# Sixteen-point Fourier stages as packed 64x64 matmuls, with the filter tables stored in halves by frequency

## The chip, the cores and the metric

The kernel runs on one core of a Trainium2 chip. Its metric is the device time of one execution in microseconds (us). The kernel before took 217.96 us, the median of three runs from 217.56 to 218.0. One execution was recorded by the hardware profiler: 218.46 us as a run, of which 216.3 us are the span from its first recorded instruction to its last. TensorE had its full clock (1.00) as the mean of that span.

## What is computed

The input x has 2048 rows of 640 values in bf16. After a layer norm the rows go two ways and meet again:

```
xn = layernorm(x)
s  = irfft2(rfft2(xn) * (w_r + 1j * w_i))                 # over both axes, 2048 x 640
g  = silu((gelu(xn @ w_gate) * (xn @ w_up)) @ w_down)     # 640 -> 1536 -> 640
out = x + s * g
```

w_r and w_i are filter tables of 2048 by 321 values. The kernel writes the Fourier transforms as matmuls with tables of sines and cosines that it makes itself.

## The kernel before, in words

The 2048 rows are numbered by 16 n2 + n1, and the long transform is split into 128 points (n2) and 16 points (n1). One *slab* is the 128 rows of one n1. The work runs in three Fourier stages beside a feed-forward network (FFN).

- **Forward stage, slab by slab.** `slab_S1` (line 490) does the 128-point transform of a slab, `slab_D` (line 507) the 640-point one along the row. `slab_D` stores the result in a buffer `ZDR` in HBM.
- **Middle stage, sixteen points and the filter.** `load_B2` (line 517) waits for all of `ZDR` and reads it back as a tile `B2` of 128 partitions by 32 positions by 321 values, in another order: the partitions now hold real or imaginary part, n1, and four quarters of the frequency. `pair_S2` (line 524) takes two of the 32 positions: two matmuls with the table `MG` (128x128, of which each row of the table uses only a part), a copy from PSUM by ScalarE into `xs`, and two multiplications by VectorE with the filter tables `W1` and `W2` into `p1` and `p2`. `pair_S2i` (line 541) goes back with four matmuls, tables `N1` and `N2`, a copy by ScalarE into `us`, and two stores into a second HBM buffer `UDR`. There are 16 such pairs. The tile `us` rotates through three buffers, so the fourth copy has to wait until the stores of the first have landed.
- **Inverse stage, slab by slab.** `load_V` (line 556) waits for all of `UDR` and reads it back in four transfers; `vfold` (line 564), `slab_S1i` (line 579) and `slab_Di` (line 591) undo the row transforms. `finish` multiplies by the gate, adds x and stores the rows.
- **The FFN.** Four groups g of 512 rows. `ffn_half` (line 646) does five matmuls of 128x512 for one tile of the gate or the up projection; a gelu on ScalarE (line 638) and a product on VectorE (line 640) follow. `down_third` (line 653) does eight matmuls of 128x320 of the down projection.

The order of every engine's instructions is written by hand. A list `back` holds the FFN in 144 *slots*, and `plan` hangs Fourier work on a slot, to be issued behind the FFN work of that slot (line 815). Slots 0 to 35 are the FFN's group 0, 36 to 71 group 1 (60 to 71 its down projection), 72 to 107 group 2 (96 to 107 down), 108 to 143 group 3. `load_B2` stands at slot 58, the first `pair_S2` at slot 66, the last `pair_S2i` and `load_V` at slot 92, the first `slab_S1i` at slot 101. The statistics for the layer norm of group 2 end at slot 24, and its Newton steps for the reciprocal root (`rsqrt4_a`, `rsqrt4_b`) stand at slot 26, on VectorE behind two gate products (line 681) of slots 25 and 26.

All plain transfers are issued by SyncE, whose queue (SPq in the profile) works strictly in the order of the program. The program uses eight semaphores for these transfers in turn, so that each transfer waits, before it is issued, until the eighth one before it has landed. The filter tables are loaded in 14 transfers over slots 10 to 42 and two copies from table to table (`w_dup`); all are issued before `load_B2`.

Of the kernel before, what the change touches and what calls it, by code (L numbers as in the profile page):

```python
# [30 lines left out]
def kernel(  # L31
# [36 lines left out]
    W1 = wts.tile([P, NH, L], BF16)  # L68
    W2 = wts.tile([P, NH, L], BF16)
# [6 lines left out]
def build(nc, env):  # L76
# [27 lines left out]
    def w_plus(i, lo):  # L104
        WT, sp = spw[i]
        for ri in range(2):
            p0 = ri * 64 + lo * 16
            nc.sync.dma_start(out=WT[p0:p0 + 16, :, :], in_=sp[:, lo * 32:lo * 32 + 32, :])

    def w_minus(i, lo):  # L110
        WT, sp = spw[i]
        if lo == 0:
            nc.sync.dma_start(out=WT[32:48, :, :], in_=sp[:, 96:64:-1, :])
        else:
            nc.sync.dma_start(out=WT[48:64, 1:NH, :], in_=sp[:, 127:96:-1, :])
            nc.sync.dma_start(out=WT[48:64, 0, :], in_=sp[:, 64, :])

    def w_dup(i):
        WT = spw[i][0]
        nc.sync.dma_start(out=WT[96:128, :, :], in_=WT[32:64, :, :])  # L120

    def w_edge(i):
        WT = spw[i][0]
        nc.gpsimd.tensor_scalar(out=WT[:, :, 0:L:320], in0=WT[:, :, 0:L:320], scalar1=0.5, scalar2=None,
                                op0=ALU.mult)
# [5 lines left out]
    MG = consts.tile([P, 2, P], BF16)  # L131
# [87 lines left out]
    def tinv_row():  # L219
        row = consts.tile([1, P], BF16)  # L220
        nc.gpsimd.memset(row[:, 0:P:2], 1.0)
        nc.gpsimd.memset(row[:, 1:P:2], -1.0)
        nc.sync.dma_start(out=Tinv[64:65], in_=row.unsqueeze(1).to_broadcast([1, NS, P]))
# [56 lines left out]
    def mg_iota():  # L280
        kr = mtile([2, 2, 2, 16], INT32, "kr")
        lc = mtile([2, 2, 2, 16], INT32, "lc")
        for ri in range(2):
            nc.gpsimd.iota(kr[:, ri, 0], pattern=[[0, 2], [1, 16]], base=0, channel_multiplier=0)
            nc.gpsimd.iota(kr[:, ri, 1], pattern=[[0, 2], [-1, 16]], base=15, channel_multiplier=0)
            nc.gpsimd.iota(lc[:, ri, 0], pattern=[[1, 2], [0, 16]], base=0, channel_multiplier=0)
            nc.gpsimd.iota(lc[:, ri, 1], pattern=[[-1, 2], [0, 16]], base=1, channel_multiplier=0)
        mg["kr"], mg["lc"] = kr, lc

    def mg_phase():  # L290
        n1_f, z_f = bits("mb", [(2, 15), (1, 1)])
# [10 lines left out]
        php0 = aff("php0", hi_f, 512.0, zc)  # L302
        php1 = aff("php1", php0, 1.0, 512.0)
        phm0 = aff("phm0", hi_f, -512.0, zc)
        phm1 = aff("phm1", phm0, 1.0, 1536.0)
        phs0 = aff("phs0", hi_f, 512.0, 1536.0)
# [3 lines left out]
        vg = mtile([2, 2, 2, 16], INT32, "vg")  # L310
        vs = mtile([4, 16], INT32, "vs")
        for ri, pm, ph in ((0, 0, php0), (1, 0, php1), (0, 1, phm0), (1, 1, phm1)):
            nc.gpsimd.tensor_scalar(out=vg[:, ri, pm], in0=kr[:, ri, pm], scalar1=n1x, scalar2=ph,
                                    op0=ALU.mult, op1=ALU.add)
        for j, ph in enumerate((phs0, phs1, phs2, phs3)):
            nc.gpsimd.tensor_scalar(out=vs[:, j, :], in0=kr[:, 0, 0, 0, :], scalar1=n1x, scalar2=ph,
                                    op0=ALU.mult, op1=ALU.add)
        mg["vgf"], mg["vs"] = vg.rearrange("p a b c d -> p (a b c d)"), vs
# [5 lines left out]
    def mg_sin():  # L324
        mg["sg"] = sg = mtile([P], FP32, "sg")
        mg["ss"] = ss = mtile([4, 16], FP32, "ss")
        nc.scalar.activation(out=sg, in_=mg["vgf"], func=ACT.Sin, bias=negpi, scale=TWO_PI / 2048.0)
        nc.scalar.activation(out=ss, in_=mg["vs"], func=ACT.Sin, bias=negpi, scale=TWO_PI / 2048.0)

    def mg_build():  # L330
        sg, ss, z_f, lo_f = mg["sg"], mg["ss"], mg["z"], lo_b
        mk = mg["kr"].rearrange("p a b c d -> p (a b c d)").bitcast(FP32)
        nc.vector.tensor_scalar(out=mk, in0=mg["lc"].rearrange("p a b c d -> p (a b c d)"), scalar1=lo_f,
                                scalar2=None, op0=ALU.is_equal)
        nc.vector.tensor_tensor(out=MG[:, 1, :], in0=sg, in1=mk, op=ALU.mult)
        nc.vector.tensor_copy(out=MG[:, 0, :], in_=MG[:, 1, :])
        lo0 = affine("lo0", lo_f, -1.0, 1.0)
        mz1 = c1("mz1")
        nc.vector.tensor_tensor(out=mz1, in0=z_f, in1=lo0, op=ALU.mult)
        mz0 = c1("mz0")  # L340
        nc.vector.tensor_tensor(out=mz0, in0=lo0, in1=mz1, op=ALU.subtract)
        for ri in range(2):
            for pm, mz in ((0, mz0), (1, mz1)):
                q0 = ri * 64 + pm * 32 + pm * 16
                nc.vector.tensor_scalar(out=MG[:, 0, q0:q0 + 16], in0=ss[:, pm * 2 + ri, :], scalar1=mz,
                                        scalar2=None, op0=ALU.mult)
        mg["MJ"] = MJ = mtile([2, P], BF16, "MJ")
        nc.vector.tensor_copy(out=MJ[:, :, 0:64], in_=MG[:, :, 64:128])
        nc.vector.tensor_scalar_mul(out=MJ[:, :, 64:128], in0=MG[:, :, 0:64], scalar1=-1.0)

    def mg_turn():
        MJ = mg["MJ"]
        pt = psB.tile([P, 4, P], BF16, tag="b")
        for k in range(2):
            nc.tensor.transpose(out=pt[:, k, :], in_=MG[:, k, :], identity=ident)
            nc.tensor.transpose(out=pt[:, 2 + k, :], in_=MJ[:, k, :], identity=ident)
# [160 lines left out]
    def load_B2():  # L517
        B2 = big.tile([P, NH, L], BF16, tag="sB", name="B2")
        zv = ZDR.rearrange("c n (a h) l -> (c n a) h l", a=4)
        for q in range(4):  # L520
            nc.sync.dma_start(out=B2[:, 8 * q:8 * q + 8, :], in_=zv[:, 8 * q:8 * q + 8, :])
        st_b["B2"] = B2

    def pair_S2(h):
        B2 = st_b["B2"]
        px = psB.tile([P, 2, 512], FP32, tag="b")
        for k in range(2):
            hi = 2 * h + k
            nc.tensor.matmul(px[:, k, 0:L], lhsT=MG[:, min(hi, 1), :], rhs=B2[:, hi, :], start=True, stop=True)  # L529
        xs = work.tile([P, 2 * L], BF16, tag="m1", bufs=2)  # L530
        nc.scalar.copy(out=xs.rearrange("p (k l) -> p k l", k=2), in_=px[:, :, 0:L])  # L531
        p1 = work.tile([P, 2 * L], BF16, tag="p1", bufs=2)
        p2 = work.tile([P, 2 * L], BF16, tag="p2", bufs=2)
        for pp, WT in ((p1, W1), (p2, W2)):
            nc.vector.tensor_tensor(out=pp, in0=xs, in1=WT[:, 2 * h:2 * h + 2, :].rearrange("p k l -> p (k l)"),  # L535
                                    op=ALU.mult)
        st_b[h] = (p1, p2)

    uv = UDR.rearrange("n (a h) f -> (n a) h f", a=4)

    def pair_S2i(h):
        p1, p2 = st_b.pop(h)
        pu = psB.tile([P, 2, 512], FP32, tag="b")
        for NM, pp, first in ((N1, p1, True), (N2, p2, False)):
            for k in range(2):
                hi = 2 * h + k
                nc.tensor.matmul(pu[:, k, 0:L], lhsT=NM[:, min(hi, 1), :], rhs=pp[:, k * L:(k + 1) * L],  # L547
                                 start=first, stop=not first)
        us = work.tile([P, 2, L], BF16, tag="m2", bufs=3)
        nc.scalar.copy(out=us, in_=pu[:, :, 0:L])  # L550
        nc.sync.dma_start(out=uv[:, 2 * h:2 * h + 2, 0:L], in_=us[0:64, :, :])
        nc.sync.dma_start(out=uv[:, 2 * h:2 * h + 2, L:D], in_=us[64:128, :, 1:320])
# [3 lines left out]
    def load_V():  # L556
        V = big.tile([P, NS, D], BF16, tag="sB", name="Vin")
        for g in range(4):
            nc.sync.dma_start(out=V[:, 4 * g:4 * g + 4, :],
                              in_=UDR.rearrange("n p f -> p n f")[:, 4 * g:4 * g + 4, :])  # L560
# [30 lines left out]
    def slab_Di(n1):  # L591
        py = psB.tile([P, 2, 512], FP32, tag="b")
        d_matmuls(py, st_c.pop(n1))
        eo = work.tile([P, 2, LP], BF16, tag="p1", bufs=2)
# [32 lines left out]
    def ffn_piece(g, t, k, c0, c1_):  # L627
# [8 lines left out]
        if k == 0:  # L636
            cur["ge"] = work.tile([P, 512], BF16, tag="ge", bufs=3, name="ge")[:, c0:c1_]
            nc.scalar.activation(out=cur["ge"], in_=ps, func=ACT.Gelu_apprx_tanh)  # L638
        else:
            nc.vector.tensor_tensor(out=uT[g][:, t, c0:c1_], in0=ps, in1=cur["ge"], op=ALU.mult)  # L640

    def ffn_part(g, t, h):
        for k in range(2):
            ffn_piece(g, t, k, h * 256, h * 256 + 256)

# [87 lines left out]
    for g, st, rs, nf in ((1, (9, 10, 11, 12), 13, ((14, 15), (16, 17))), (2, (18, 20, 22, 24), 26, ((27, 28), (30, 32))),  # L733
                          (3, (33, 35, 37, 39), 40, ((41, 42), (45, 46)))):
# [14 lines left out]
    for sl, it in f_units.items():  # L749
        put(sl, *it)  # L750
    filt = [(w_plus, 0, 0), (w_minus, 0, 0), (w_minus, 0, 1), (w_minus, 1, 0), (w_minus, 1, 1), (w_plus, 0, 1),
            (w_dup, 0), (w_dup, 1), (w_plus, 1, 0), (w_plus, 1, 1)]
    for n1, item in enumerate(filt):
        put([sl for sl, it in f_units.items() if it == (slab_D, n1)][0], *item)
    put(50, w_edge, 0)
    put(53, w_edge, 1)
    put(2, vt_iota, 1)
    put(12, tinv_angle, 1)
# [8 lines left out]
    put(z_end, load_B2)  # L767
    put(58, mg_build)
    put(61, mg_turn)
    sb = z_end + 8  # L770
    for h in range(NS):
        down = back[sb][0] is down_third
        put(sb, pair_S2, h)
        if h > 0:
            put(sb + (0 if down else 1), pair_S2i, h - 1)
        sb += 1 if down else 2
    put(sb, pair_S2i, NS - 1)
    put(sb, load_V)
    vs0 = sb + 9
# [35 lines left out]
    for s, b in enumerate(back):  # L815
        b[0](*b[1:])
        for it in plan[s]:
# [32 lines left out]
```

## Time and profile before

| | us |
|---|---|
| median of three runs | 217.96 |
| the profiled execution as a run | 218.46 |
| its span | 216.3 |
| TensorE busy in the span | 203.4 |
| VectorE, ScalarE, GpSimd busy | 144.0, 129.3, 14.4 |
| first matmul of the middle stage (`px`, line 529) | starts at 101.5 |
| last matmul of the middle stage (`pu`, line 547) | starts at 143.0 |
| first full group of the inverse stage (`pv`, line 583) | starts at 153.54 |
| bytes moved by DMA | 31.77 MB |

All times inside the profile count from the start of the span. PE is TensorE, PEld its weight loads, DVE is VectorE, ACT is ScalarE, POOL is GpSimd, SPq is the queue of SyncE that issues the transfers. A matmul's recorded duration includes its way through the array; matmuls overlap, so the pace of a row of matmuls is read from the starts in the timeline, not from the duration of one. The chain of waits is followed back from the last instruction: at each step to what released it.

### The profile page before, as it was taken

How to read it: one execution, taken by the hardware profiler on the slowest of the kernel's cores; microseconds unless marked ns; L12 is line 12 of the kernel's file. 1: busy time of each engine (PE TensorE's matmuls, PEld its weight loads, DVE VectorE, ACT ScalarE, POOL GpSimd, SP SyncE). 2: the span in 40 equal slices, each digit the busy share in tenths (PEclk: the TensorE clock that was granted, in tenths of full speed). 3: DMA queues.
4: the chain of work that ended last, by engine and by line, in shares of the span. 5: the costliest groups of instructions: out<-in, count | busy, mean ns of one | idle time of the engine just before them, and what ended most of it. 6: DMA issues, size and time to landing. Idle time of an engine off the chain costs nothing.

```text
span 216.3 us, 4227 instructions
## 1 busy us (share of the span) xinstructions
PE 203.4 (94%) x1504; PEld 131.8 (61%) x1504; DVE 144.0 (67%) x478; ACT 129.3 (60%) x215; POOL 14.4 (7%) x44
## 2 busy tenths in 40 slices
PE   0699999998999999999999999999999999999993
PEld 0389984676665555567665555557676656666773
DVE  8888988956987852352665544543667888894442
ACT  7556567594764945533785656651467666765721
POOL 8000203800000000000000000000000000000000
PEclk9999999999999999999999999999999999999999
DMA  5999999999999996329542222233943433322131
GB/s 163 344 363 361 340 161 105 142 149 134 128 203 212 159 210 112 75 62 334 185 91 62 62 58 48 47 79 102 371 150 95 120 121 100 112 66 64 28 108 50
DMA packets 35253, 31.77 MB, mean 147 GB/s; under 512 B 10336, under 2 KB 34016, under 8 KB 35040
## 3 DMA queue, kind: packets, MB, share of 16 engines
q1 hardware_dynamic: 35232, 31.50, 64.1%
q8 instruction: 12, 0.20, 0.4%
q14 instruction: 9, 0.07, 0.1%
HBM read 20.34 MB, written 7.87 MB: 130 GB/s over the span
## 4 chain that ended last, share of the span: by engine, by line
PE 81%; DVE 6%; ACT 5%; DMA 5%; issue 1%; SPq 0%; ACTq 0%; DVEq 0%
PE psg L634 22%; PE psu L634 22%; PE psg L650 9%; PE psu L650 9%; PE pu L547 4%; PE pv L583 2%; PE py L503 2%; PE py L502 2%; PE px L529 2%; DMA Vin<-UDR 2%; PE pd L502 2%; PE pd L503 2%; PE pz L494 2%; DMA UDR<-us 2%; PE pw L273 1%
## 5 line engine op out<-in xcount | busy, mean ns | idle before, releaser
L634 PE MATMUL psg<-xnT,Wg 128*128 128x512 bf16 (+1 forms) x275 | 61.4, 354 | 0.0
L634 PE MATMUL psu<-xnT,Wu 128*128 128x512 bf16 (+1 forms) x275 | 60.9, 352 | 0.0
L650 PEld LDWEIGHTS <-uT 128*128 128x128 bf16 x396 | 37.5, 98 | 13.7 <-DVE uT L640 0.2
L640 DVE TENSOR_TENSOR uT<-psu,ge 128x512 bf16<-128x512 f32 (+1 forms) x55 | 33.9, 616 | 17.4 <-PE psu L634 17.0
L638 ACT ACTIVATE ge<-psg 128x512 bf16<-128x512 f32 (+1 forms) x55 | 29.9, 544 | 19.1 <-PE psg L634 16.9
L634 PEld LDWEIGHTS <-Wg 128*128 128x128 bf16 x275 | 25.9, 99 | 18.4 <-issue 0.6
L634 PEld LDWEIGHTS <-Wu 128*128 128x128 bf16 x275 | 26.3, 98 | 17.8
L650 PE MATMUL psg<-Wd,uT 128*128 128x320 bf16 (+1 forms) x204 | 30.8, 295 | 0.0
L650 PE MATMUL psu<-Wd,uT 128*128 128x320 bf16 (+1 forms) x192 | 29.0, 295 | 0.0
L535 DVE TENSOR_TENSOR p<-xs,W 128x642 bf16<-128x642 bf16 x32 | 14.4, 492 | 17.5 <-ACT xs L531 17.3
L585 ACT CAST vs<-pv 128x640 bf16<-128x640 f32 x16 | 11.1, 692 | 9.6 <-PE pv L583 9.6
L550 ACT CAST us<-pu 128x642 bf16<-128x642 f32 x16 | 11.2, 698 | 7.4 <-PE pu L547 7.4
L512 ACT CAST zd<-pd 128x644 bf16<-128x644 f32 x16 | 11.1, 694 | 6.0 <-PE pd L503 4.0
L373 DVE BATCH_NORM_STATS2 st<-X 128x6 f32<-128x320 bf16 x32 | 13.9, 477 | 0.0
L496 ACT CAST Z<-pz 128x640 bf16<-128x640 f32 x16 | 11.0, 689 | 4.0 <-PE pz L494 4.0
L607 DVE TENSOR_TENSOR Yall<-Yall,G 128x640 bf16<-128x640 bf16 (+2 forms) x21 | 8.7, 412 | 6.2 <-ACT G L686 5.8
L595 ACT ACTIVATE eo<-py 128x644 bf16<-128x644 f32 x16 | 11.3, 707 | 1.8 <-PE py L503 1.5
L531 ACT CAST xs<-px 128x642 bf16<-128x642 f32 x16 | 11.0, 690 | 2.2 <-PE px L529 1.3
L502 PE MATMUL pd<-FT,Z 128*128 128x161 bf16 x64 | 10.4, 233 | 1.4 <-ACT Tfwd L232 1.4
L547 PE MATMUL pu<-p,N 128*128 128x321 bf16 x64 | 11.6, 301 | 0.0
L681 DVE SCALAR_TENSOR_TENSOR G<-th,psg 128x320 bf16<-128x320 f32 x12 | 5.8, 481 | 7.1 <-ACT th L680 7.1
L502 PE MATMUL py<-FT,vs 128*128 128x161 bf16 x64 | 10.5, 233 | 0.0
(150 smaller groups left out, 242.6 us busy)
## 6 DMA issues: line engine op xcount, KB each, us to landing
ZDR<-zd SPq DMA_DIRECT2D x16, 160.5 KB, 6.2
B<-ZDR SPq DMA_DIRECT2D x4, 642.0 KB, 6.1
Vin<-UDR SPq DMA_DIRECT2D x4, 640.0 KB, 6.3
xt<-in_A_x_dram SPq DMA_DIRECT2D x16, 160.0 KB, 2.5
Wg<-in_B_w_gate_dram SPq DMA_DIRECT2D x4, 480.0 KB, 7.5
Wu<-in_B_w_up_dram SPq DMA_DIRECT2D x4, 480.0 KB, 8.5
X<-in_A_x_dram SPq DMA_DIRECT2D x3, 640.0 KB, 9.0
Wd<-in_B_w_down_dram SPq DMA_DIRECT2D x1, 1920.0 KB, 13.9
```

The lines of the kernel that those rows point to most:

```text
L373: nc.vector.bn_stats(out=st[:, k, :], in_=xr[:, k, :])
L502: nc.tensor.matmul(o, lhsT=lhs[:, 2 * b + k, :], rhs=FT[:, 2 * b + k, :], start=True, stop=False)
L512: nc.scalar.copy(out=zd.rearrange("p c (m b) -> p c m b", b=2), in_=natural(pd))
L535: nc.vector.tensor_tensor(out=pp, in0=xs, in1=WT[:, 2 * h:2 * h + 2, :].rearrange("p k l -> p (k l)"), op=ALU.mult)
L547: nc.tensor.matmul(pu[:, k, 0:L], lhsT=NM[:, min(hi, 1), :], rhs=pp[:, k * L:(k + 1) * L], start=first, stop=not first)
L550: nc.scalar.copy(out=us, in_=pu[:, :, 0:L])
L585: nc.scalar.copy(out=vs, in_=pv)
L595: nc.scalar.activation(out=eo.rearrange("p c (m b) -> p c m b", b=2), in_=natural(py), func=ACT.Copy, scale=(2.0 if n1 >= 12 else 1.0) / ( ...
L634: nc.tensor.matmul(ps, lhsT=WT[:, c, t * P:(t + 1) * P], rhs=xnT[g][:, c, c0:c1_], start=(c == 0), stop=(c == 4))
L638: nc.scalar.activation(out=cur["ge"], in_=ps, func=ACT.Gelu_apprx_tanh)
L640: nc.vector.tensor_tensor(out=uT[g][:, t, c0:c1_], in0=ps, in1=cur["ge"], op=ALU.mult)
L650: nc.tensor.matmul(ph, lhsT=uT[g][:, t, j * P:(j + 1) * P], rhs=Wd[:, t, c0:c1_], start=(t == 0), stop=(t == NT - 1))
```

## The change

The two sixteen-point transforms no longer use 128x128 tables with zeros in them, but quarters of the array: 64 rows by 64 columns, four at a time with a different quarter each. The 32 positions are regrouped as 2 x 8 positions and two halves, `lo` is now the upper or lower half of the partitions, and one *quad* of four positions replaces a pair. The filter tables become two tiles each, `W1[0]`, `W1[1]`, `W2[0]`, `W2[1]`; in them the real and imaginary rows of the plus and minus frequencies take every fourth partition. The second tiles (b = 1) are loaded behind `load_B2`. The same bytes move in more transfers: 30 loads and copies of filter tables over slots 10 to 48 and 28 behind `load_B2`, eight transfers for `B2` instead of four, four stores of `us` per quad (64 in all) instead of two per pair (32), five for `Vin` instead of four.

The core of the diff ("..." marks what is left out; the making of `MG`, `N1`, `N2` changes with it, and its work gets smaller):

```
-    W1 = wts.tile([P, NH, L], BF16)
-    W2 = wts.tile([P, NH, L], BF16)
+    W1 = [wts.tile([P, 2, 8, L], BF16, name=f"W1{b}") for b in range(2)]
+    W2 = [wts.tile([P, 2, 8, L], BF16, name=f"W2{b}") for b in range(2)]
...
+    def w_rows(i, b, half, ri, pm):
+        q0 = half * 64 + ri * 2 + pm
+        return spw[i][0][b][q0:q0 + 61:4]
+
+    def w_plus(i, b, lo, half):
+        r = lo * 32 + b * 16 + half * 8
         for ri in range(2):
-            p0 = ri * 64 + lo * 16
-            nc.sync.dma_start(out=WT[p0:p0 + 16, :, :], in_=sp[:, lo * 32:lo * 32 + 32, :])
+            nc.sync.dma_start(out=w_rows(i, b, half, ri, 0)[:, lo], in_=spw[i][1][:, r:r + 8, :])
+    def w_minus(i, b, lo, half):
...
+    def w_dup(i, b, half):
+        nc.sync.dma_start(out=w_rows(i, b, half, 1, 1), in_=w_rows(i, b, half, 0, 1))
...
     def load_B2():
...
         for q in range(4):
-            nc.sync.dma_start(out=B2[:, 8 * q:8 * q + 8, :], in_=zv[:, 8 * q:8 * q + 8, :])
+            b, s = q // 2, q % 2 * 4
+            for lo in range(2):
+                nc.sync.dma_start(out=B2[lo * 64:lo * 64 + 64, b, :, s:s + 4, :], in_=zv[lo][:, b, :, s:s + 4, :])
...
-    def pair_S2(h):
+    def quad_S2(j):
...
-        for k in range(2):
-            hi = 2 * h + k
-            nc.tensor.matmul(px[:, k, 0:L], lhsT=MG[:, min(hi, 1), :], rhs=B2[:, hi, :], start=True, stop=True)
+        for lo in range(2):
+            rows = slice(lo * 64, lo * 64 + 64)
+            for half in range(2):
+                nc.tensor.matmul(px[half * 64:half * 64 + 64, lo, 0:L], lhsT=MG[rows, min(j + half, 1), :],
+                                 rhs=B2[rows, j // 8, half, j % 8, :], start=True, stop=True)
...
-        p1 = work.tile([P, 2 * L], BF16, tag="p1", bufs=2)
+        p1 = work.tile([P, 2, L], BF16, tag="p1", bufs=3)
...
+            nc.vector.tensor_tensor(out=pp, in0=xs, in1=WT[j // 8][:, :, j % 8, :], op=ALU.mult)
...
-    def pair_S2i(h):
+    def quad_S2i(j):
...
         for NM, pp, first in ((N1, p1, True), (N2, p2, False)):
+            for half in range(2):
+                rows = slice(half * 64, half * 64 + 64)
+                for lo in range(2):
+                    cols = slice(lo * 64, lo * 64 + 64)
+                    nc.tensor.matmul(pu[cols, half, 0:L], lhsT=NM[rows, min(j, 1), cols], rhs=pp[rows, lo, :],
+                                     start=first, stop=not first)
         us = work.tile([P, 2, L], BF16, tag="m2", bufs=3)
         nc.scalar.copy(out=us, in_=pu[:, :, 0:L])
-        nc.sync.dma_start(out=uv[:, 2 * h:2 * h + 2, 0:L], in_=us[0:64, :, :])
-        nc.sync.dma_start(out=uv[:, 2 * h:2 * h + 2, L:D], in_=us[64:128, :, 1:320])
+        for lo in range(2):
+            to = uv[lo][:, j // 8, :, j % 8, :]
+            nc.sync.dma_start(out=to[:, :, 0:L], in_=us[lo * 64:lo * 64 + 32, :, :])
+            nc.sync.dma_start(out=to[:, :, L:D], in_=us[lo * 64 + 32:lo * 64 + 64, :, 1:320])
...
         for g in range(4):
+            for k in ((0, 2), (2, 4)) if g == 0 else ((0, 4),):
...
-            nc.scalar.activation(out=cur["ge"], in_=ps, func=ACT.Gelu_apprx_tanh)
+            late.append(lambda: nc.scalar.activation(out=ge, in_=ps, func=ACT.Gelu_apprx_tanh))
...
-    for g, st, rs, nf in ((1, (9, 10, 11, 12), 13, ...), (2, (18, 20, 22, 24), 26, ...), (3, (33, 35, 37, 39), 40, ...)):
), (2, (18, 20, 22, 24), 24, ...), (3, (33, 35, 37, 39), 39, ...)):
...
+    def filt(b):
+        plus = [(w_plus, i, b, lo, half) for half in range(2) for i in range(2) for lo in range(2)]
+        minus = [(w_minus, i, b, lo, half) for half in range(2) for i in range(2) for lo in range(2)]
+        dup = [(w_dup, i, b, half) for half in range(2) for i in range(2)]
+        return minus[:4] + plus[:4] + dup[:2] + minus[4:] + plus[4:] + dup[2:]
...
+    for k, item in enumerate(filt(0)):
+        put(d_slot[k * 12 // 20], *item)
...
     put(z_end, load_B2)
+    for k, item in enumerate(filt(1)):
+        put(z_end + 1 + k // 2, *item)
...
+    for j in range(NS):
+        put(sb, quad_S2, j)
+        if j > 1:
+            put(sb, quad_S2i, j - 2)
+        sb += 2 if sb % 3 == 1 else 1
+    put(sb, quad_S2i, NS - 2)
+    put(sb + 1, quad_S2i, NS - 1)
+    sb += 1
     put(sb, load_V)
-    vs0 = sb + 9
+    vs0 = sb + 11
...
         b[0](*b[1:])
+        if not any(it[0] is quad_S2 for it in plan[s]):
+            flush()
         for it in plan[s]:
             it[0](*it[1:])
+        flush()
```

Quads stand at slots 66, 67, 69, 70 and so on to 88, two in every three slots; `quad_S2i` of a quad is issued behind `quad_S2` of the second quad after it, so the first stands at slot 69 and the last two at 90 and 91. `load_V` moves from slot 92 to 91, the first `slab_S1i` from 101 to 102. In a slot with a quad the gelu of the slot's FFN work is issued behind the quad's copies on ScalarE, elsewhere it stays where it was.

## Prediction

> **What bounds the kernel now.** I read the chain of waits first, then the groups by line, then TensorE's timeline at the edges of the middle stage, then SyncE's queue.
>
> ```profile
> PE 203.4 (94%) x1504; PEld 131.8 (61%) x1504; DVE 144.0 (67%) x478; ACT 129.3 (60%) x215; POOL 14.4 (7%) x44
> PE 81%; DVE 6%; ACT 5%; DMA 5%; issue 1%; SPq 0%; ACTq 0%; DVEq 0%
> L547 PE MATMUL pu<-p,N 128*128 128x321 bf16 x64 | 11.6, 301 | 0.0
> ```
>
> TensorE carries 81% of the chain; SyncE's queue none. So a matmul saved shortens the end, as long as no other engine takes its place. In the timeline a pair's matmuls start 0.28 us (`px`, two) and 0.55 us (`pu`, four) before what follows, 0.137 us each: the middle stage owns 16 x 0.82 = 13.1 us. TensorE waits at two places that matter here:
>
> ```profile
> 54.54 0.23 PE L502 MATMUL pd<-FT,Z 128*128 128x161 bf16 x1 [1.39 <-ACT Tfwd L232]
> ```
>
> ```profile
> 153.07 0.23 PE L583 MATMUL pv<-Tinv,f 128*128 128x128 bf16 x1
> 153.54 0.59 PE L583 MATMUL pv<-Tinv,f 128*128 128x128 bf16 x4 [0.25 <-DVE f L443]
> ```
>
> The second shows how tight the way from the last store through `load_V` is: `vfold` starts the moment `Vin` lands (152.58), and TensorE waits for it. SyncE's queue in that stretch, where columns are start, duration, and the tile views of its stores with minimum, median and maximum in ns:
>
> ```profile
> 96.69 1.94 SPq L521 DMA_DIRECT2D B<-ZDR  x4
> 104.94 0.70 SPq L551 DMA_DIRECT2D UDR<-us  x1
> 105.69 0.60 SPq L552 DMA_DIRECT2D UDR<-us  x1
> ...
> 142.46 0.57 SPq L551 DMA_DIRECT2D UDR<-us  x1
> 143.08 0.61 SPq L552 DMA_DIRECT2D UDR<-us  x1
> 144.14 0.57 SPq L551 DMA_DIRECT2D UDR<-us  x1
> 144.76 0.61 SPq L552 DMA_DIRECT2D UDR<-us  x1
> 148.31 2.36 SPq L559 DMA_DIRECT2D Vin<-UDR  x4
> ```
>
> ```profile
> L551 SPq DMA_DIRECT2D UDR<-us x16: 574/574/704, 104.9 to 144.1; - x16
> L552 SPq DMA_DIRECT2D UDR<-us x16: 599/606/608, 105.7 to 144.8; - x16
> ```
>
> ```profile
> L609 SPq DMA_DIRECT2D out_dram<-Yall x21: 332/343/344, 160.7 to 213.7; - x21
> ```
>
> To issue one store of `us` costs SyncE 0.59 us, with the gap to the next start 0.635 us. A pair needs 1.27 us of SyncE and comes every 2.98 us: the queue is idle over half the time. That is the reserve which the change spends.
>
> **The change part by part.**
>
> *Newton steps of group 2 to slot 24.* VectorE sits idle for 2.42 us up to 48.97, waiting for a tanh; the thirteen Newton steps, 50.30 to 52.6, now stand behind it and take 2.35 us. Moved to slot 24 they fit that gap. ScalarE's norm and the copy `Tfwd` behind it, which TensorE awaits at 54.54, come earlier. Gain 1.39 us; the least is 0, if another wait is late next. I take 1.39, so `load_B2` starts at 96.69 - 1.39 = 95.3. The same slot shifts for groups 1 and 3 answer to no wait of TensorE: nothing.
>
> *Matmuls.* A quad has 4 + 8 matmuls of 64x64 by 321 columns in place of 2 + 4 of 128x128. No row shows a quarter of the array. If four run together, a quad takes three times 0.137 = 0.41 us: 16 x 0.41 = 6.6 us saved. If each takes the array for itself, 12 x 0.137 = 1.64 us: 13.1 us lost. A lone way through the array costs more than its pace: duration 0.301 against 0.137, so 0.164 us to drain. With a drain at each end of a quad's matmuls it takes 0.41 + 0.33 = 0.74 us and the saving is 1.3 us. I take 0.55, between packed and drained; both ends stay for the range. The Trainium skill speaks on both sides: "TensorE: Matmul & The Clock Gate", Part 3, has tiles in different quarters run at the same time, 4 ns apart; "TensorEngine Tiling (Array Packing)", Key Properties, says that a change of the tiling mode drains TensorE, and its Restrictions that column tiling loses the fast weight load. No row here shows either; by the first alone the saving would be the 6.6 us, by the second about the 1.3 us or less.
>
> *Filter tables up to slot 48.* Fourteen more transfers on SyncE, about 0.48 us each (L108: 0.93 for two), 6.7 us in a queue that idles between its `ZDR` stores; transposed rows for group 1 are issued by 42 and used at 61. Nothing, in either direction by a microsecond at most.
>
> *VectorE and ScalarE.* The filter products read `W` in two runs of 321 instead of one of 642. Line 535 takes 0.492 us; 321 values with an odd length (line 598) take 0.33, so no slower rate shows. If it fell to half, 32 x 0.3 = 10 us, VectorE (53% busy from 110 to 140) would hide it, as the products now have two quads' time. The late gelu moves by two copies of 0.69 us; its bank is wanted again four slots later: nothing. POOL's table steps and `w_edge` (0.46 us) have no one waiting.
>
> *SyncE behind `load_B2`: the first new wait.* The built queue has, in this order, 8 loads of `B2`, 28 transfers for `W1[1]` and `W2[1]`, and only then the first store of `us`. Each transfer waits for the eighth before it to land. `B2` landed up to 8.9 us after the last issue (98.0), at 106.9, now 105.5: until then only eight filter transfers are out. The other 20 at 0.48 us take 9.6 us: the first store goes out at 115.1. With no such wait it is 95.3 + 36 x 0.465 = 112.0; neither bound is near the 104 or so at which the first `us` is ready. Three buffers of `us` carry ScalarE through three quads. The fourth copy needs the first quad's stores landed: 115.1 + 3 x 0.635 + 2.2 = 119.2, done at 119.9. It holds ScalarE, thus the gelus behind it, and the PSUM tile, thus `quad_S2i` of the next quad at slot 75, where TensorE arrives at 100.1 + 9 x 1.087 + 7 x 0.5 = 113.4. TensorE stands for some 6.5 us.
>
> *Stores: the second new wait.* Four per quad at 0.635 us are 2.54 us of SyncE; TensorE needs (3 x 1.087 + 2 x 0.55)/2 = 2.18 us per quad. SyncE is the slower one, and it is already late. Cost of one: the nearest rows are L551 and L552 themselves (64 partitions; now 32); the copy from 32 partitions (line 120) took 0.64. The row against it is the store of 128 partitions, 0.343. I take 0.635; the low end is 0.385 with its gap. The last of 64 goes out at 115.1 + 63 x 0.635 = 155.1, lands 2.9 later (median 2.2; the last one before, 144.76 to 148.31, 3.5): 158.0. First piece of `Vin`, half as large: between 2.5 (`xt`, 160 KB) and 4.27 (148.31 to 152.58): 3.2, so 161.2. `vfold` to `pv` 0.96: 162.2. TensorE alone would be there at 120 + 27 x 1.087 + 11 x 0.55 = 155.4: it waits.
>
> **Sum.** `pv` starts at 162.2 instead of 153.54, with one slot more (1.09 us) behind it: 162.2 - 153.54 - 1.09 = +7.6 us. From there the inverse stage and the FFN run as before. 218.46 + 7.6 = 226.0 us for an execution like the profiled one, which is 0.5 above the median of the runs; I keep 226.
>
> **Rivals.**
>
> *The stores are cheap (0.385 to 0.48 us), the first one still late.* TensorE restarts at 119.5 and arrives by its own work at 119.5 + 29.4 + 6 = 154.9, against 154.63 before with the same work done: +0.3; with drained matmuls +2.4. 218.8 to 221. For it: the 128-partition row. Against it: L551 moves half of that and costs more.
>
> *The queue keeps up: faster.* One mechanism, SyncE's issue in the middle stage. If the 28 transfers flow without the wait for landings (first store 112.0) and a store costs 0.385, TensorE restarts at 112.0 + 1.2 + 2.2 + 0.7 = 116.1; with packed matmuls 116.1 + 29.4 + 4.5 = 150.0, so -4.6: 214. It decides from a store below some 0.45 us. For it: TensorE's 81% of the chain. Against: every row of `us`.
>
> *The quarters don't run together.* 1.64 us a quad: 120 + 29.4 + 11 x 1.64 = 167.4, +12.8: 231. For it: no row has shown packing. Against: the four use different rows and columns.
>
> **How the numbers follow.** The forecast, SyncE the bound (222 to 229.5): 0.60. Cheap stores (218 to 222): 0.17. The queue keeps up (213 to 217.5): 0.15. No packing (229 to 234): 0.08. The range of 217.5 to 229.5 leaves out about 0.2. A measurement of this kernel can't tell less than 0.2% (0.4 us) from no change. Faster: 0.15 and a little of the cheap stores, 0.18; same 0.03; slower 0.79.
>
> **What would show it.** SyncE's queue without a gap from 95 to the last store near 155; the first store near 115; ScalarE's copy `us` waiting for the `UDR` transfers, once for several us, then shortly at each quad; TensorE idle near slot 75 and again before `pv`. The wait of 1.39 us for `Tfwd` gone. Matmuls of `px` in fours that start almost together would show packing; starts 0.137 us apart would show none. I'm wrong if the first store leaves before 108 or the stores take 0.4 us each.

## The result, and the profile after

| | before | after |
|---|---|---|
| median of 4 runs, us | 217.76 (217.56 to 218.0) | 227.95 (227.79 to 228.41) |
| profiled execution as a run, us | 218.46 | 228.07 |
| its span, us | 216.3 | 225.8 |
| mean granted clock of TensorE | 1.00 | 0.97 |

The ratio is 1.0471, with a 95% interval of 1.045 to 1.0493: the change made the kernel 4.7% slower, 10.2 us between the medians and 9.5 us between the two spans. The forecast was 226.0.

The page of the changed kernel first: the engines' busy time, the rows of slices for TensorE and for its clock, the chain of waits by engine, and the two groups that matter.

```profile
PE 199.8 (88%) x1582; PEld 125.6 (56%) x1600; DVE 143.9 (64%) x475; ACT 127.4 (56%) x215; POOL 14.1 (6%) x40
PE   0799999999999999999800599999999999999994
PEclk9999999999999999999985599999999999999999
PE 78%; SPq 8%; DMA 7%; DVE 2%; issue 2%; ACT 1%; POOL 0%; ACTq 0%; POOLq 0%
L552 ACT CAST us<-pu 128x642 bf16<-128x642 f32 x16 | 11.2, 699 | 16.9 <-DMA UDR<-us 16.1
L549 PE MATMUL pu<-p,N 64*64 64x321 bf16 x128 | 7.8, 320 | 14.2 <-ACT us L552 14.2
```

TensorE has less to do (199.8 us instead of 203.4), yet its share of the chain falls from 81% to 78%. What came in is SyncE's queue: 8%, where it had 0%. In the row of slices there is one hole, at slices 20 to 22 (counted from 0), and in the row below it the clock falls to half in the same place. The two groups name the hole: `pu` waited 14.2 us for the copy `us`, and `us` waited 16.1 us for its stores to land.

SyncE's queue in that stretch, start and duration first:

```profile
92.88 5.22 SPq L520 DMA_DIRECT2D B<-ZDR  x8
...
102.94 6.46 SPq L111 DMA_DIRECT2D W<-in_A_w_r_dram  x4
109.45 2.50 SPq L111 DMA_DIRECT2D W<-in_A_w_i_dram  x4
...
122.24 0.53 SPq L555 DMA_DIRECT2D UDR<-us  x1
...
155.59 0.43 SPq L556 DMA_DIRECT2D UDR<-us  x1
157.43 2.50 SPq L565 DMA_DIRECT2D Vin<-UDR  x5
```

Between the eight loads of `B2` and the first store of `us` the queue holds nothing but filter tables. Up to 109.45 they go at the pace at which `B2` lands (each waits for the eighth transfer before it), and from there to 122.24 at 0.64 us each, 20 of them. In those last 12.8 us the queue has no gap, while the share of the DMA engines reads 0.49 (1.06 from 100 to 106): there the issues set the pace, not the bytes. The first `us` had been cast since 104.3; its store left 18 us later.

The timelines of ScalarE (first line) and TensorE around the hole:

```profile
125.51 0.69 ACT L552 CAST us<-pu 128x642 bf16<-128x642 f32 x1 [15.51 <-DMA UDR<-us]
```

```profile
126.26 0.75 PE L549 MATMUL pu<-p,N 64*64 64x321 bf16 x8 [14.25 <-ACT us L552]
127.34 1.91 PE L639 MATMUL psg<-xnT,Wg 128*128 128x512 bf16 x4 [0.33 <-issue]
```

The fourth copy of `us` needs the first of the three buffers, whose stores had not even been issued. The last of them lands at 125.37, the copy follows at 125.51, TensorE at 126.26. And there is a second cost in the last line: four matmuls of 512 columns span 1.91 us, where a group of five takes 1.24 elsewhere. The windows of 1 us show it (third number from the right: the granted clock):

```profile
115.00:116.00 1.00, 0.00 (x0) 0.00 (x0) 0.00 (x0) 0.00 (x0) 0.00 (x0) 1.00 0.46 111
116.00:117.00 1.00, 0.00 (x0) 0.00 (x0) 0.00 (x0) 0.00 (x0) 0.00 (x0) 0.88 0.55 125
117.00:118.00 1.00, 0.00 (x0) 0.00 (x0) 0.00 (x0) 0.00 (x0) 0.00 (x0) 0.50 0.54 156
...
130.00:131.00 1.00, 1.00 (x8) 0.41 (x5) 0.51 (x2) 1.00 (x3) 0.00 (x0) 0.79 0.20 43
```

The clock is 1.00 up to 116.8, 0.50 from there on, and full again only at 130.4. TensorE works at half pace from 126.26 to there: some 2 us.

Ahead of the hole the changed kernel is faster. `px` begins at 98.6 instead of 101.5. And behind it nothing waits: the store issued at 155.59 and `Vin` at 157.43 are in time for `pv`, which has no wait before it:

```profile
164.53 0.44 PE L588 MATMUL pv<-Tinv,f 128*128 128x128 bf16 x5
```

### The profile page after: what moved, and what is told of

The parts are those of the page before. It is cut to its first block, busy times and chain, and to the rows that moved or that the text cites. A ratio compares the mean times of both kernels' runs of the same rounds, so it can differ in the third digit from the quotient of the medians.

```text
span 225.8 us, 4510 instructions
## 1 busy us (share of the span) xinstructions
PE 199.8 (88%) x1582; PEld 125.6 (56%) x1600; DVE 143.9 (64%) x475; ACT 127.4 (56%) x215; POOL 14.1 (6%) x40
## 4 chain that ended last, share of the span: by engine, by line
PE 78%; SPq 8%; DMA 7%; DVE 2%; issue 2%; ACT 1%; POOL 0%; ACTq 0%; POOLq 0%
PE psg L639 22%; PE psu L639 22%; PE psg L663 9%; PE psu L663 8%; DMA B<-ZDR 5%; SPq L111 3%; PE pz L491 2%; PE pv L588 2%; PE pd L500 2%; PE py L500 2%; PE py L499 2%; PE pd L499 2%; SPq L520 2%; PE pu L549 2%; PE pw L278 1%
## 5 line engine op out<-in xcount | busy, mean ns | idle before, releaser
L639 PE MATMUL psg<-xnT,Wg 128*128 128x512 bf16 (+1 forms) x263 | 60.3, 356 | 1.0 <-issue 0.5
L639 PE MATMUL psu<-xnT,Wu 128*128 128x512 bf16 (+1 forms) x269 | 60.1, 352 | 0.4 <-issue 0.3
L644 ACT ACTIVATE ge<-psg 128x512 bf16<-128x512 f32 (+1 forms) x55 | 30.0, 546 | 18.2 <-PE psg L639 16.5
L639 PEld LDWEIGHTS <-Wu 128*128 128x128 bf16 x275 | 25.4, 98 | 19.8 <-issue 2.2
L552 ACT CAST us<-pu 128x642 bf16<-128x642 f32 x16 | 11.2, 699 | 16.9 <-DMA UDR<-us 16.1
L549 PE MATMUL pu<-p,N 64*64 64x321 bf16 x128 | 7.8, 320 | 14.2 <-ACT us L552 14.2
L549 PEld LDWEIGHTS <-N 64*64 64x64 bf16 x128 | 3.8, 111 | 15.5 <-issue 15.3
L693 ACT ACTIVATE th<-psu 128x320 f32<-128x320 f32 x12 | 5.3, 439 | 9.4 <-PE psu L663 9.3
## 6 DMA issues: line engine op xcount, KB each, us to landing
Wd<-in_B_w_down_dram SPq DMA_DIRECT2D x1, 1920.0 KB, 13.7
```

The lines of the kernel that those rows point to most:

```text
L549: nc.tensor.matmul(pu[cols, half, 0:L], lhsT=NM[rows, min(j, 1), cols], rhs=pp[rows, lo, :], start=first, stop=not first)
L639: nc.tensor.matmul(ps, lhsT=WT[:, c, t * P:(t + 1) * P], rhs=xnT[g][:, c, c0:c1_], start=(c == 0), stop=(c == 4))
L644: late.append(lambda: nc.scalar.activation(out=ge, in_=ps, func=ACT.Gelu_apprx_tanh))
```

## The experiments

Four theories were to be told apart. **A**: SyncE's order of issue, filter tables ahead of the stores, each at its price. **B**: the pieces of the change themselves: the quarters of the array, their drains, the smaller transfers. **C**: the bytes moved behind `B2`, or the landing of `B2`, whatever the number of issues. **D**: the three buffers of `us`. In the first four runs the kernel before took 218.37 us on the same chip, in the next four 218.37 again, in the last three 218.03.

### All tables ahead of `load_B2`

```diff
-    for k, item in enumerate(filt(0)):
-        put(d_slot[k * 12 // 20], *item)
+    for k, item in enumerate(filt(0) + filt(1)):
+        put(d_slot[k * 15 // 40], *item)
...
-    for k, item in enumerate(filt(1)):
-        put(z_end + 1 + k // 2, *item)
```

> All 40 filter items (58 transfers) are issued ahead of load_B2, so that the first store of us is the next transfer behind the eight of B2. Theory A (the time is lost because 28 filter transfers stand ahead of the first store in SyncE's queue): the stall of 14.25 us at slot 75 goes, and with it the half clock behind it; 36 slots at 1.085 and 16 quads at 0.63 us from px at 98.6 give pv at 147.7 instead of 164.5, so about 211 us, up to 214 if the earlier transfers hold up the stores of ZDR. Rival B (the quarters of the array, their drains or the smaller transfers of B2 and us are what costs): the stall stays or shows elsewhere, 222 us or more.

Measured: 216.61 us, ratio 0.9915 (0.9888 to 0.9942): faster than before. The hole is gone, so A holds and B, which had it stay, does not. But 211 was expected, 214 at most. TensorE's timeline shows where the rest is, and below it one line of the windows, in which the third number from the right is the granted clock:

```profile
99.86 0.32 PE L529 MATMUL px<-B,MG 64*64 64x321 bf16 x2 [1.26 <-DMA B<-ZDR]
101.37 0.32 PE L529 MATMUL px<-B,MG 64*64 64x321 bf16 x2 [1.19 <-DMA B<-ZDR]
```

```profile
102.00:105.00 3.00, 3.00 (x15) 1.36 (x14) 1.42 (x4) 1.56 (x3) 0.00 (x0) 0.50 1.07 229
```

The same queue now makes the next thing late. The table transfers stand ahead of the last `ZDR` stores; the last one is issued at 92.91 instead of 90.55, the loads of `B2` start at 95.71 instead of 92.88, and `px` waits for them, 2.45 us in two pieces. Right behind these the clock is at 0.50 for 3.4 us (101.94 to 105.35), which costs 1.7 us more. Together that is 4 us, most of what is missing.

### Fewer transfers, same place

```diff
-        r = lo * 32 + b * 16 + half * 8
-        for ri in range(2):
-            nc.sync.dma_start(out=w_rows(i, b, half, ri, 0)[:, lo], in_=spw[i][1][:, r:r + 8, :])
+        r = b * 16 + half * 8
+        sp = spw[i][1].rearrange("k (q r) l -> k q r l", q=4)
+        nc.sync.dma_start(out=w_rows(i, b, half, lo, 0), in_=sp[:, 0:2, r:r + 8, :])
```

One transfer now carries both halves of a table's rows; the bytes are the same, the issues behind `B2` are 20 instead of 28.

> The plus rows of a filter table come in one transfer for both lo instead of two: 20 transfers behind load_B2 instead of 28, the same bytes. Theory A (count of issues at 0.637 us each sets the first store): first store 8 x 0.637 = 5.1 us earlier, at about 117.1, stall 9.2 us, 222.9 us in all. Rival C (bytes behind B2 or the landing of B2 set it, not the count): first store within 1.5 us of 122.2, 226.5 to 228 us.

Measured: 225.78 us, ratio 1.0319 (1.0283 to 1.0354). SyncE's queue and TensorE's wait:

```profile
93.81 5.29 SPq L520 DMA_DIRECT2D B<-ZDR  x8
...
118.83 0.58 SPq L555 DMA_DIRECT2D UDR<-us  x1
```

```profile
123.77 0.75 PE L549 MATMUL pu<-p,N 64*64 64x321 bf16 x8 [10.88 <-ACT us L552]
```

With the same bytes and eight issues fewer the first store goes 3.4 us earlier, not the 5.1 of eight times 0.64: `B2` began 0.9 later, and the merged transfers wait for its landing all the same. The stall shortens by the same 3.4. So the number of issues sets it, as A has it, and C, which left the first store where it was within 1.5 us, falls; but the landing of `B2` remains a part of the delay. The time falls by 2.2 us only, where 5 were expected: `px` begins 0.75 later, so TensorE is back just 2.5 us earlier, and the clock still halves, until 128.5.

### Sixteen buffers of `us`

```diff
+        st_b["US"] = big.tile([P, NS, 2, L], BF16, tag="sX", name="US")
...
-        us = work.tile([P, 2, L], BF16, tag="m2", bufs=3)
+        us = st_b["US"][:, j]
```

> Sixteen buffers for us instead of three, in the space that X leaves; the filter tables stay behind load_B2. Theory A: ScalarE no longer waits for stores, but the second half of the tables, whose last copies are issued at 121, is wanted by quad 8 at slot 78 near 114: the stall moves there and shrinks to 6 to 8 us, and the stores begin at 122 with a backlog, so that Vin is late too: 219 to 223 us. Rival D (the depth of three buffers alone is the cause): no stall, 211 to 214 us.

Measured: 226.71 us, ratio 1.0369 (1.0339 to 1.0398). The copy waits for no store any more, and the kernel gains 1.2 us of 10; 219 to 223 were expected. TensorE's two new waits, in its timeline:

```profile
125.06 0.48 PE L550 MATMUL pu<-p,N 64*64 64x321 bf16 x4 [4.17 <-DVE p L537]
...
159.98 0.29 PE L589 MATMUL pv<-Tinv,f 128*128 128x128 bf16 x1 [4.90 <-DVE f L440]
```

First the ninth quad's product `p` waits for the second half of the tables: its last copies are issued at 121.24 and 121.87, GpSimd's edge step on the first of the two tables, which waits for their landing, runs from 124.15 to 124.47, and `p` starts at 124.51 (the profile puts this wait down to a store's landing; the edge step is what ends just ahead of it). Then the 64 stores, begun only at 122.56, hold up `Vin` and with it `pv`. This is the second wait of the prediction, which the kernel with three buffers did not have because its long first wait had let the queue catch up. D falls: depth moves the wait, the queue makes it. The clock halves twice here, at 123.2 and at 157.3.

### All tables early, and fewer

The two edits above together, the tables over 13 shards instead of 15.

> All filter transfers ahead of load_B2, as in the run with the tables early, and each row range of the plus tables for both q-halves in one transfer, so 40 issues instead of 56, spread so that the last stands three shards of D earlier. Theory (SyncE's order of issue sets the time): ZDR(15) is issued near 90.5 us again and B starts near 92.9, not 95.7; the two px waits for B of 1.26 and 1.19 us and the half clock after them (about 1.7 us) go; 216.6 less 2.5 less 1.7 gives 212 us. Rival (the DMA engines, not the order of issue, make B late: the same bytes are moved): px still waits 2 us or more and the time stays near 216.

Measured: 212.3 us, ratio 0.9731 (0.9704 to 0.9758). Of TensorE's waits above 0.12 us only the one at the start is left, and the clock is 1.00. SyncE's queue: `B2` at 94.04 (in between the two runs), the first store at 105.53.

### The second half of the tables on GpSimd's queue

```diff
+    def weng(b):
+        return (nc.sync, nc.gpsimd)[b]
...
-            nc.sync.dma_start(out=w_rows(i, b, half, ri, 0)[:, lo], in_=spw[i][1][:, r:r + 8, :])
+            weng(b).dma_start(out=w_rows(i, b, half, ri, 0)[:, lo], in_=spw[i][1][:, r:r + 8, :])
...
     for k, item in enumerate(filt(1)):
-        put(z_end + 1 + k // 2, *item)
+        put(30 + k, *item)
```

> The second half's 20 filter items issued from GpSimd's queue in slots 30 to 49, everything else as in the changed kernel. Theory (SyncE's order of issue sets the time): SyncE holds nothing between load_B2 and the first store, so the first us store goes as soon as the tile is cast, the 14 us stall at pu and the half clock are gone, and the time is 211 to 213 us. Rival: transfers started by GpSimd cost more than the ones of SyncE (no row of GpSimd's DMAs in this case), or slow VectorE beside them, so that tables or B come late all the same: 216 or more.

Measured: 211.93 us, ratio 0.9722 (0.9687 to 0.9757). The page, then SyncE's queue, then one of GpSimd's rows (minimum, median and maximum in ns):

```profile
PE 199.2 (95%) x1600; PEld 125.2 (60%) x1600; DVE 144.0 (69%) x475; ACT 127.4 (61%) x215; POOL 28.0 (13%) x68
PE   0699999999999999999999999999999999999993
PEclk9999999999999999999999999999999999999999
PE 95%; DVE 2%; ACT 1%; issue 0%; POOL 0%; POOLq 0%
```

```profile
92.84 5.22 SPq L523 DMA_DIRECT2D B<-ZDR  x8
104.40 0.34 SPq L558 DMA_DIRECT2D UDR<-us  x1
```

```profile
L114 POOL DMA_DIRECT2D W<-in_A_w_r_dram x8: 483/489/512, 43.3 to 55.5; - x8
```

This is the changed kernel with 28 issues moved to another queue, and from slots 59 to 68 forward to 30 to 49. This run by itself doesn't tell the other queue from the earlier time; in the run with all tables early the hole went on the old queue too. Both answer the question: between `B2` and the first store SyncE has nothing, the store goes as soon as `us` is cast, TensorE carries 95% of the chain and has no hole. The matmuls, the copies and the tables are those of the changed kernel, so B falls too. A table load costs GpSimd 0.48 to 0.55 us to issue and lands in 6.2 to 6.5 us (SyncE: 0.56 to 0.63 in this run, and 3.2 to 4.0), and TensorE waits for none.

A second measurement of this kernel, as the base of two others:

> The kernel with the second half of the tables on GpSimd's queue once more, as the base of the next two and for a narrower interval: 211.9 us, TensorE without a wait from 7 us to the end.

212.68 us, ratio 0.9745 (0.9724 to 0.9766). The profiles of the two differ by 0.9 us in span, and 0.7 of that has arisen by 19 us, where the last transpose `pt` of the start stands (18.2 and 18.9): the start of the kernel varies by that much.

### Pieces of the change by themselves

**The Newton steps alone**, in the kernel before. (The second added line is the one that the diff in "The change" shows broken.)

```diff
-    for g, st, rs, nf in ((1, (9, 10, 11, 12), 13, ...), (2, (18, 20, 22, 24), 26, ...),
-                          (3, (33, 35, 37, 39), 40, ...)):
+    for g, st, rs, nf in ((1, (9, 10, 11, 12), 12, ...), (2, (18, 20, 22, 24), 24, ...),
+                          (3, (33, 35, 37, 39), 39, ...)):
```

> The kernel before with one part of the change: the Newton steps in slots 12, 24 and 39 instead of 13, 26 and 40. If the wait of 1.39 us for Tfwd is the whole early gain: 216.4 us (ratio 0.9935). If the 2.9 us by which the changed kernel reaches its first px earlier come from these slots: 214.9 (0.986). If another wait takes its place: 217.8.

Measured: 218.33 us, ratio 0.9988 (0.9968 to 1.0007): no gain that can be measured. The same kernel once more, for its profile:

> The kernel before with only the Newton steps moved to slots 12, 24 and 39, a second look for its profile. The wait of 1.39 us for Tfwd is gone. If the time did not move because another wait took its place, the profile shows that wait on TensorE between 57 us and the end, of about 1.4 us: at zd for ZDR's landing or at px for B. If instead the wait was on no path that sets the end, px begins about 1.4 us earlier and the difference is lost between px and pv.

217.3 us in one run. TensorE's timeline:

```profile
89.33 0.23 PE L502 MATMUL pd<-FT,Z 128*128 128x161 bf16 x1 [1.18 <-ACT zd L512]
```

The wait for `Tfwd` is gone and this one has come: ScalarE's copy `zd` waited 3.9 us for the landing of earlier `ZDR` stores. In this kernel they land in 6.5 us (median), in the changed kernel in 2.6. The reverse trial, **the Newton steps put back** to slots 13, 26 and 40 in the kernel with the tables on GpSimd's queue:

> The kernel with the second half of the tables on GpSimd's queue, with the Newton steps put back to slots 13, 26 and 40: this part of the change undone alone, in a kernel in which TensorE waits for nothing. Theory (the 1.39 us wait for Tfwd is on TensorE's own path, and in the kernel before its gain was taken by a wait for ZDR's landing that the new table and store layout has removed): the wait near 54 us is back and the time is 1.0 to 1.5 us longer, about 213.2. Rival (moving the Newton steps gains nothing wherever it stands, as the run with this part alone in the kernel before gave): same as its base within 0.4 us.

Measured: 214.25 us, ratio 0.9822 (0.9799 to 0.9845), 1.6 us more than its base, and the wait is back in its old place:

```profile
54.54 0.23 PE L502 MATMUL pd<-FT,Z 128*128 128x161 bf16 x1 [1.35 <-ACT Tfwd L240]
```

So this part gains 1.6 us in the kernel with the new tables, beside which the `ZDR` stores land sooner, and nothing that can be measured in the kernel before. That the sooner landing is the reason is read from the timelines and was not tried by itself.

**The quarters apart**: in the kernel with all tables early and fewer, `quad_S2i` one slot later than the `quad_S2` it stood beside, so that TensorE changes to the 64-row shape three times for two quads instead of twice.

```diff
         if j > 1:
-            put(sb, quad_S2i, j - 2)
+            put(sb + 1, quad_S2i, j - 2)
```

> The previous run with all filter transfers early and fewer, with each quad's inverse stage (pu) one slot later than the forward stage of the quad it stood beside, so that in two consecutive slots out of three px and pu of different quads still stand in one slot, and 3 visits to the 64-row shape instead of 2 are made for every 2 quads. Theory that each visit to the smaller tile costs a fixed 0.2 us, however many matmuls it holds: 8 visits more, +1.6 us against the run it is made from. Rival (no fixed cost per visit; the 0.09 us of lead-in is all): +0.3 us at most beside the longer tail of one slot.

Measured: 213.42 us, ratio 0.9787 (0.9751 to 0.9824), 1.1 us more than its base (1.7 between the two spans). TensorE's timeline over two quads, first the base and then this run:

```profile
108.86 1.25 PE L639 MATMUL psu<-xnT,Wu 128*128 128x512 bf16 x5
110.05 0.33 PE L529 MATMUL px<-B,MG 64*64 64x321 bf16 x4
110.21 0.45 PE L549 MATMUL pu<-p,N 64*64 64x321 bf16 x8
110.58 1.25 PE L639 MATMUL psg<-xnT,Wg 128*128 128x512 bf16 x5
...
113.39 1.25 PE L639 MATMUL psg<-xnT,Wg 128*128 128x512 bf16 x5
```

```profile
109.03 1.25 PE L639 MATMUL psu<-xnT,Wu 128*128 128x512 bf16 x5
...
112.34 1.25 PE L639 MATMUL psu<-xnT,Wu 128*128 128x512 bf16 x5
113.53 0.33 PE L529 MATMUL px<-B,MG 64*64 64x321 bf16 x4
113.79 1.25 PE L639 MATMUL psg<-xnT,Wg 128*128 128x512 bf16 x5
```

Each fence goes from one group of five matmuls to the third behind it, over two quads: 4.53 us in the base and 4.76 with the quarters apart, 0.23 us for one more visit. From `px` to `pu` behind it is 0.16 us, little more than the 0.137 of one matmul of 321 columns: the four run together. But where `px` stands alone (last three lines), it comes 1.19 us behind the group's start, where a group takes 1.09, and the next group 0.26 behind it: 0.36 us for four matmuls. A visit has a fixed price of about 0.2 us, on the side of the first theory. The Trainium skill has a possible cause, without a price ("TensorEngine Tiling (Array Packing)", Key Properties: a change of the tiling mode drains TensorE). The price agrees with it; that it is the drain, and not for example the first weight load of a visit, is not shown.

**Fewer transfers on both queues**: the edit of the second run, in the kernel with the tables on GpSimd's queue.

> The kernel with the second half of the tables on GpSimd's queue and, besides, the rows of the plus tables for both q-halves in one transfer (8 issues fewer on each queue). If TensorE waits for nothing in its base, fewer issues can't move the end: 211.9, within 0.4 us of the base. If the issues still cost something (SyncE's order ahead of ZDR and B, or GpSimd beside VectorE), up to 1 us less.

Measured: 211.81 us, ratio 0.9717 (0.9697 to 0.9736), the best version of all, 2.8% faster than before. Its base, measured beside it, took 0.9 us more, but 211.93 the first time, and 0.7 of the difference between the two profiles stand by 19 us already, in the start. That the eight issues on each queue matter is not shown.

## Why the prediction was right, and where it was not

The sign, the mechanism of the first wait and the order of the size were right: SyncE's strict queue, filled with table transfers between `B2` and the first store. The time was near (226.0 against 227.95 and, for the profiled execution, 228.07), but two of its steps were wrong by some 7 us each, in opposite directions: that the number came so near is luck.

**The Newton steps** (predicted gain 1.39 us). The wait for `Tfwd` went, and undoing this part costs 1.6 us. The gain up to `px` was larger, 2.9 us. By the starts of `pz` in the two kernels it comes in three steps: 1.0 us before the first `pz` (22.67 and 21.64), 0.4 from the fifth to the sixth, 1.6 from the eighth to the ninth, where the wait for `Tfwd` stood. The middle one is a wait that the prediction had put at nothing, for the normalized rows of group 1:

```profile
36.32 0.22 PE L494 MATMUL pz<-Tfwd,f 128*128 128x128 bf16 x1
36.70 0.47 PE L494 MATMUL pz<-Tfwd,f 128*128 128x128 bf16 x4 [0.16 <-DVE f L443]
```

It is gone in the changed kernel, where all five start at 35.29, and back in the run with the Newton steps put back (36.38 and 36.75). Of the 1.0 us at the start, `pw` makes 0.56, as VectorE's wrap of the first table (1.09 us before, beside an iota of GpSimd) takes 0.64 with GpSimd's work out of its way, which is a reading of the timelines and was not tried by itself; the other 0.5 us falls within what the start varies by.

**Matmuls** (predicted 0.55 us a quad between 0.41 and 0.74). Measured in the kernel with no stall: 0.09 + 0.16 + 0.38 = 0.63 us, against 0.82 before. The four quarters do run together, and a fixed price stands in the way of the full gain. The 0.2 us saved per quad make 3.1 us in all, the part that the change is for.

**SyncE behind `load_B2`** (predicted: first store at 115.1, stall 6.5 us). The mechanism was right in each link: the semaphores' wait for `B2`, three buffers, ScalarE's copy, `pu` at slot 75. The sizes were too small twice. The queue passed `B2`'s landing at 109.45 instead of 105.5, although its loads had begun 2.4 us earlier: eight smaller loads cost 0.60 to 0.66 us each to issue, where four had cost 0.42, and the last landed 11.4 us behind its issue (why so late was not tried). And the 20 transfers behind it took 0.64 us each instead of the 0.48 that was read from `w_plus` before. Together 3.9 + 3.2 = 7.1 us: first store at 122.24. TensorE arrived at 112.0 instead of 113.4. Stall: 14.25 us.

**Stores** (predicted 0.635 us each, so that SyncE bounds the rest and `pv` waits some 7 us). This step failed: the term was mis-sized.

```profile
L555 SPq DMA_DIRECT2D UDR<-us x32: 303/421/527, 122.2 to 155.1; - x32
L556 SPq DMA_DIRECT2D UDR<-us x32: 419/427/1660, 122.8 to 155.6; - x32
```

A store of 32 partitions takes 0.42 us and starts every 0.47, four in 1.9 us against TensorE's 2.2 per quad; the queue caught up and no wait stood before `pv`. The prediction had chosen the nearest rows, its low end of 0.385 was nearer. Its own last sentence said that it is wrong if the stores take 0.4 us: in this step it was.

**The half clock.** The prediction left it out, though it had TensorE idle for 6.5 us. It costs 2 us here and 1.7 in the run with the tables early. The Trainium skill has the rule ("TensorE: Matmul & The Clock Gate", Part 1: half clock after an idle window of some 3.4 us, free-running). The changed kernel agrees, as its clock fell 4.8 us into the stall. Three other runs don't fit the rule's words, and the measurement decides: the clock fell 1.9 us into the stall of the run with fewer transfers, 2.3 us into each of the two waits of the run with sixteen buffers, and in the run with the tables early after two waits of 1.26 and 1.19 us with a little work between them. In the 3.41 us before these falls TensorE had been busy for 1.50, 1.09, 1.15 and 0.96 us. A stretch of that length need not be idle throughout.

The sum, step by step for `pv`, predicted at 162.2: TensorE back at 126.26 instead of about 120, +6.3; the half clock and the dearer quads on the way from there, +2.9; no wait before `pv`, -6.8. That gives 164.6; it stands at 164.53.

**The rivals.** That the quarters don't run together is excluded by the 0.16 us from `px` to `pu`. That the queue keeps up is what the run on GpSimd's queue made true: its 211.9 us are below the 214 of that rival, since the part ahead of `px` gained more, and since TensorE doesn't stop at all, where that rival still had it restart at 116.1 after an arrival at 113.4. The cheap stores with a late first one came nearest to what happened, with the wait twice as long as it had it. In the kernel without the stall, the spans' gain of 6.3 us over before is about 3.0 ahead of `px`, 3.1 for the quads and the 0.25 us wait at `pv`.

## What to carry to other kernels

A queue that issues in order is a resource with a price per transfer. Before transfers are moved behind a load, list all that stands between them and the next store on that queue, at the duration of the new shape, and look for the buffer that the store must free. A loss of this kind is not the change's own: the same matmuls with their tables on an idle engine's queue gave 2.8% where the queue as written lost 4.7%.

And when a stall is predicted, the time at half clock behind it belongs in the sum; when a wait is removed, look for the one just behind it, as the Newton steps gained nothing until the stores landed sooner.

## What the runs showed of the hardware

- What a transfer costs SyncE to issue differs with its shape and doesn't follow its bytes: 0.42 us for a store of 32 partitions by 1284 or 1276 bytes, 0.57 to 0.61 for the store of 64 with twice the bytes, 0.34 for the store of 128 partitions by 1280 with four times, 0.56 to 0.61 for table rows set into every fourth partition.
- Where filter loads wrote into 16 neighbouring partitions (before), they landed in 7.8 to 9.4 us; into every fourth partition, a quarter of the bytes each, in 2.5 to 2.8 (medians). And `ZDR` stores beside them landed in 2.6 us instead of 6.2. Which of size and pattern does it was not tried.
- Half clock can come early in a wait, or behind short ones: 1.9 us into one of 10.9, 2.3 us into waits of 4.2 and 4.9, and after two of 1.26 and 1.19. In the five cases it lasted 3.4, 6.8, 6.8, 13.7 and 13.7 us: once, twice and four times 3.41.
- A visit to the 64x64 shape costs about 0.2 us, whether it holds four matmuls (0.36 us in all) or twelve (0.63).
